# SwiGLU feed-forward on one core: the last store, 128 rows by 128 columns, split by rows over two issuing queues

## The chip, the cores and the metric

The kernel runs on one core of a Trainium2 chip. The metric is device time in microseconds (us) of one execution; the median over several runs is used. A core has engines that run side by side, each with its own queue of instructions: TensorE (PE in the profile) for matrix products, VectorE (DVE), ScalarE (ACT), GpSimd (POOL) and SyncE (SP). SyncE and ScalarE issue the data transfers (DMAs) here; the 16 DMA engines of the core move the data. Engines wait for each other by counting semaphores.

## The reference

```python
B, S, D, F = 1, 2048, 512, 1376        # all bfloat16

def reference(x, w_gate, w_up, w_down):
    g = silu(x @ w_gate)
    u = x @ w_up
    return (g * u) @ w_down            # out: 1 x 2048 x 512
```

## The kernel before

The 2048 tokens are worked on in four chunks of 512, the hidden dimension F in ten blocks of 128 and a rest of 96. Tokens lie along the free dimension of `xT_sb`, so that the first two products come out transposed, hidden units on the 128 partitions. Weights are loaded in slabs by SyncE, the first by ScalarE, in an order written out by hand. At the start SyncE (`loads_on_sync`, L123) and ScalarE (`loads_on_scalar`, L119) issue their first loads at the same time.

For each chunk and block TensorE makes the gate and the up product in two of the eight PSUM banks (L324); ScalarE takes silu of the first (L288), VectorE multiplies by the second into `hT_sb` (L296). The rests of 96 are handled in groups "X" and "Y" of their own (L404).

Then comes the down product. The 16 output tiles of 128 tokens and 512 columns are made in four groups of four (`strips`, L419, matmuls at L442). The last group is finished tile by tile in the loop at L469, matmuls at L481. A tile's bank is copied to one of eight buffers `o_sb`, by VectorE (L300) or ScalarE (L288), in turns, and stored from there to `out_dram` (L257).

The very last tile, `at == NST - 1`, is cut by columns into three groups: 0 to 383 (`LASTA` = 384), 384 to 447 (`LASTB` = 448) and 448 to 511. ScalarE copies the first, VectorE the other two. Two stores carry the tile out: columns 0 to 383 by ScalarE behind its own copy, and columns 384 to 511 by SyncE behind VectorE's last copy. All other output stores are SyncE's.

Planning code makes a list `stores`; each entry has the owner ("S" or "A"), the tile, the columns, the buffer, and the engine and count of the copy to wait for. `store_tiles` (L253) goes through the list for one owner: wait for the copy, issue the DMA, which raises `s_out[ob]` by 16 when it has landed. `n_store[ob]` counts the stores of a buffer, for two uses: a copy into a buffer waits until the buffer's earlier stores have landed, and SyncE ends the program with waits for all of them (L262 and L263). ScalarE's stores come after all its copies (L289), at the end of its queue.

Of the kernel before, what the change touches and what calls it, by code (L numbers as in the profile page):

```python
# [14 lines left out]
def bass_standalone__swiglu_ffn__prompt_kernel(nc, x, w_gate, w_up, w_down, out):  # L15
    _, S, D = x.shape
    F = w_gate.shape[1]
    P = 128
# [7 lines left out]
    NST = S // P  # L26
    LASTA = 384
    LASTB = 448
# [22 lines left out]
    with ExitStack() as es:  # L51
# [15 lines left out]
        o_sb = [sb(f"o_sb{i}", [P, D], BF16) for i in range(NOS)]  # L67
# [13 lines left out]
        s_out = [sem(f"s_out{i}") for i in range(NOS)]  # L81
# [34 lines left out]
        def out_rows(t):  # L116
            return of[t * P:(t + 1) * P, :]
# [35 lines left out]
        def add_group(kind, **what):  # L153
            g = dict(kind=kind, at=len(groups), bank=banks[len(groups) % NB], readers=[], **what)
            groups.append(g)
            return g

        def add_op(eng, g, **what):
            n_read[eng] += 1
            op = dict(g=g, at=n_read[eng], **what)  # L160
            (act_ops if eng == "A" else dve_ops).append(op)
            g["readers"].append((eng, op["at"]))
            return op

        def tview(i, dk):
            return banks[KD * i + dk][:, 0:P // 2].bitcast(BF16)
# [47 lines left out]
        for i in range(NXN):  # L214
            for dk in range(KD):
                eng = "DA"[dk % 2]
                op = add_op(
                    eng, dict(readers=[]), kind="copy", ready=(s_X, KD * i + dk + 1),
                    out=xT_sb[:, dk, i * P:(i + 1) * P], src=tview(i, dk), stored=(None, 0),
                )  # L220
# [8 lines left out]
        NO = len(groups)  # L229
        stores = []  # L230
        n_store = [0] * NOS
        tiles = [c * TPC + q for q in range(TPC) for c in ORDER]
        for at, t in enumerate(tiles):
            ob = at % NOS
            need = 16 * n_store[ob]
            parts = [(0, D)] if at < NST - 1 else [(0, LASTA), (LASTA, LASTB), (LASTB, D)]
            for c0, c1 in parts:
                g = add_group("O", t=t, c0=c0, c1=c1)
                eng = "A" if at % 2 == 1 and c0 == 0 else "D"
                op = add_op(  # L240
                    eng, g, kind="copy", out=o_sb[ob][:, c0:c1], src=g["bank"][:, 0:c1 - c0],
                    stored=(s_out[ob], need),
                )
                if c1 in (LASTA, D):
                    own = "A" if c1 == LASTA else "S"
                    stores.append((own, t, LASTA if c0 == LASTB else c0, c1, ob, eng, op["at"]))
                    n_store[ob] += 1


        def ready(op):  # L250
            return op["ready"] if "ready" in op else (s_P, op["g"]["at"] + 1)

        def store_tiles(eng, own):  # L253
            for o, t, c0, c1, ob, copied, n in stores:
                if o == own:
                    eng.wait_ge(s_A if copied == "A" else s_D, n)
                    eng.dma_start(out_rows(t)[:, c0:c1], o_sb[ob][:, c0:c1]).then_inc(s_out[ob], 16)  # L257

        def on_sync(sp):
            loads_on_sync(sp)  # L260
            store_tiles(sp, "S")
            for i in range(NOS):  # L262
                sp.wait_ge(s_out[i], 16 * n_store[i])  # L263
# [11 lines left out]
        def on_scalar(act):  # L275
            loads_on_scalar(act)
            act.activation(adummy[:, 0:4], zero_c, ACT.Silu)  # L277
            for op in act_ops:
                act.wait_ge(*ready(op))
                if op["kind"] == "silu":  # L280
                    if op["free"]:
                        act.wait_ge(s_D, op["free"])
                    fn = ACT.Silu
                else:
                    if op["stored"][1]:
                        act.wait_ge(*op["stored"])
                    fn = ACT.Copy
                act.activation(op["out"], op["src"], fn).then_inc(s_A, 1)  # L288
            store_tiles(act, "A")  # L289
# [230 lines left out]
```

## Time and profile before

| | us |
|---|---|
| median of 3 runs | 119.98 |
| lowest and highest run | 119.94 and 120.01 |
| the profiled execution, its time | 119.89 |
| its span, first to last instruction | 118.6 |
| TensorE busy | 115.9 (98% of the span) |
| VectorE busy | 38.0 |
| ScalarE busy | 35.1 |

The span is what the profile's rows lie in; the execution's own time is 1.29 us longer than it. The granted clock of TensorE was 1.000 throughout. All rows come from the one profiled execution; times in them count from the start of the span. "SPq" and "ACTq" are the DMA issues of SyncE and ScalarE: the length in such a row is what the issue takes on the issuing engine's queue, not the time until the data has landed.

### The profile page before, as it was taken

The page shows a single profiled execution, that of the slowest core. Times are in us where ns is not written, and L with a number is a line of the kernel's source. Part 1 is how long each engine was busy: PE and PEld are TensorE (multiplying, and loading weights), DVE is VectorE, ACT ScalarE, POOL GpSimd, SP SyncE. Part 2 cuts the span into 40 slices and gives each one's busy share as a digit, 9 for nine tenths or more (in the row PEclk, how much of TensorE's full clock was granted, in tenths as well). Part 3 has the DMA queues.
Part 4 walks back from the last instruction along what each step waited for, and adds up shares of the span by engine and source line. Part 5 has one row for each costly group of instructions (what it writes and reads, how often), then busy time and mean ns, then how long its engine had stood idle before and what let it go on. Part 6 is the DMA issues. An engine that isn't in the chain of part 4 may idle for free.

```text
span 118.6 us, 2344 instructions
## 1 busy us (share of the span) xinstructions
PE 115.9 (98%) x1019; PEld 59.7 (50%) x1019; DVE 38.0 (32%) x60; ACT 35.1 (30%) x62; POOL 1.1 (1%) x7
## 2 busy tenths in 40 slices
PE   7999999999999999999999999999999999999993
PEld 2788444444444444444444444444444445885442
DVE  0206542444433444324444244360000044003321
ACT  3407334353244272343263432330000033003021
POOL 1000000000000000000000000010000000000000
PEclk9999999999999999999999999999999999999999
DMA  3999999991000000000000000000000017200612
GB/s 87 290 186 336 296 161 221 268 357 25 0 6 0 0 0 0 0 3 3 0 0 6 0 0 0 0 0 6 0 6 0 0 57 237 70 0 6 202 64 88
DMA packets 17642, 8.83 MB, mean 74 GB/s; under 512 B 10624, under 2 KB 17632, under 8 KB 17632
## 3 DMA queue, kind: packets, MB, share of 16 engines
q1 hardware_dynamic: 16816, 8.33, 27.3%
q10 hardware_dynamic: 816, 0.36, 1.1%
q8 instruction: 8, 0.13, 0.5%
q14 instruction: 2, 0.02, 0.0%
HBM read 4.75 MB, written 2.10 MB: 58 GB/s over the span
## 4 chain that ended last, share of the span: by engine, by line
PE 98%; DVE 0%; issue 0%
PE bank L324 62%; PE bank L442 25%; PE bank L481 7%; PE bank L356 2%; PE bank L404 2%; PE bank L365 1%; DVE o_sb L300 0%
## 5 line engine op out<-in xcount | busy, mean ns | idle before, releaser
L324 PE MATMUL bank<-xT_sb,w_sb 128*128 128x512 bf16 (+2 forms) x384 | 73.3, 352 | 0.1
L324 PEld LDWEIGHTS bank<-xT_sb,w_sb 128*128 128x128 bf16 x384 | 36.2, 98 | 36.8 <-DMA w_sb<-in_w_gate_dram 0.3
L296 DVE TENSOR_TENSOR hT_sb<-sg_sb,bank 128x512 bf16<-128x512 f32 x40 | 27.5, 688 | 40.2 <-PE bank L324 39.3
L288 ACT ACTIVATE sg_sb<-bank 128x512 f32<-128x512 f32 x40 | 23.9, 597 | 40.6 <-PE bank L324 40.5
L442 PE MATMUL bank<-wd_sb,hT_sb 32*128 32x512 bf16 x496 | 29.0, 374 | 0.0
L442 PEld LDWEIGHTS bank<-wd_sb,hT_sb 32*128 32x128 bf16 x496 | 15.2, 93 | 11.6 <-issue 0.4
L300 DVE CAST o_sb<-bank 128x512 bf16<-128x512 f32 (+1 forms) x10 | 5.7, 595 | 31.1 <-PE bank L442 25.9
L288 ACT ACTIVATE o_sb<-bank 128x512 bf16<-128x512 f32 (+1 forms) x8 | 4.3, 582 | 33.6 <-PE bank L442 27.9
L481 PE MATMUL bank<-wd_sb,hT_sb 128*128 128x512 bf16 (+2 forms) x56 | 8.1, 304 | 0.0
L481 PEld LDWEIGHTS bank<-wd_sb,hT_sb 128*128 128x128 bf16 x56 | 4.2, 98 | 4.2 <-issue 0.4
L442 PE MATMUL bank<-wd_sb,hy_sb 32*128 32x512 bf16 (+1 forms) x32 | 5.0, 371 | 0.0
L296 DVE TENSOR_TENSOR hx_sb<-sgx_sb,bank 32x512 bf16<-32x512 f32 x4 | 2.8, 692 | 3.5 <-ACT sgx_sb L288 3.5
L288 ACT ACTIVATE sgx_sb<-bank 32x512 f32<-32x512 f32 x4 | 2.4, 588 | 4.5 <-PE bank L324 4.5
L356 PE MATMUL bank<-const-bfloat16-1.0 128*128 128x512 bf16 (+1 forms) x9 | 2.8, 463 | 0.8 <-PEq L505 0.8
L442 PE MATMUL bank<-wd_sb,hx_sb 32*128 32x512 bf16 (+1 forms) x16 | 3.0, 371 | 0.0
L288 ACT ACTIVATE sgy_sb<-bank 64x512 f32<-64x512 f32 x4 | 2.4, 590 | 0.1
L356 PEld LDWEIGHTS bank<-const-bfloat16-1.0 128*128 128x128 bf16 x9 | 1.0, 128 | 2.2 <-issue 2.2
L300 DVE COPY xT_sb<-bank 128x128 bf16<-128x128 bf16 x4 | 0.8, 222 | 4.3 <-PE bank L365 4.3
L404 PE MATMUL bank<-xT_sb,w_sb 128*64 128x512 bf16 x16 | 1.9, 382 | 0.0
L442 PEld LDWEIGHTS bank<-wd_sb,hy_sb 32*128 32x128 bf16 x32 | 1.6, 93 | 0.6
L277 ACT ACT_TABLE_LOAD x1 | 1.3, 1283 | 1.9 <-issue 1.9
L404 PEld LDWEIGHTS bank<-xT_sb,w_sb 128*64 128x64 bf16 x16 | 0.8, 109 | 1.0 <-DVE hT_sb L296 0.4
(15 smaller groups left out, 6.6 us busy)
## 6 DMA issues: line engine op xcount, KB each, us to landing
out_dram<-o_sb SPq DMA_DIRECT2D x15, 128.0 KB, 1.8
wd_sb<-in_w_down_dram SPq DMA_DIRECT2D x1, 1280.0 KB, 7.3
w_sb<-in_w_gate_dram SPq DMA_DIRECT2D x1, 480.0 KB, 5.5
w_sb<-in_w_up_dram SPq DMA_DIRECT2D x1, 448.0 KB, 6.2
w_sb<-in_w_gate_dram SPq DMA_DIRECT2D x1, 384.0 KB, 4.3
w_sb<-in_w_up_dram SPq DMA_DIRECT2D x1, 384.0 KB, 4.7
w_sb<-in_w_up_dram SPq DMA_DIRECT2D x2, 128.0 KB, 3.2
w_sb<-in_w_gate_dram SPq DMA_DIRECT2D x1, 256.0 KB, 3.6
```

What stands on the lines that cost most here:

```text
L277: act.activation(adummy[:, 0:4], zero_c, ACT.Silu)
L288: act.activation(op["out"], op["src"], fn).then_inc(s_A, 1)
L296: ins = dve.tensor_tensor(op["out"], op["a"], op["b"], ALU.mult)
L300: ins = dve.tensor_copy(op["out"], op["src"])
L324: return pe.matmul(bank[:, n0:n1], lhsT=w_sb[:, dk, col:col + P], rhs=xT_sb[:, dk, c * SC + n0:c * SC + n1], start=(dk == 0), stop=(dk == ...
L356: pe.matmul(banks[NB - 1][:, 0:width], lhsT=ones_w, rhs=ones_m[:, 0:width], start=True, stop=True)
L365: pe.matmul(tview(i, dk), lhsT=xn_sb[:, i, dk * P:(dk + 1) * P], rhs=ident[:, :], start=True, stop=True, is_transpose=True,).then_inc(s_X, 1)
L404: ins = pe.matmul(g["bank"][y0:y1, :], lhsT=w_sb[:, dk, YC0:YC0 + 64], rhs=xT_sb[:, dk, c * SC:(c + 1) * SC], start=(dk == 0), stop=(dk == ...
L442: ins = pe.matmul(g["bank"][:, 0:c1 - c0], lhsT=h, rhs=wd_sb[r0:r0 + SR, w, c0:c1], start=(start and fk == fks[0]), stop=(stop and fk == f ...
L481: ins = pe.matmul(g["bank"][:, 0:c1 - c0], lhsT=h, rhs=w, start=(last and fk == 0), stop=(fk == (NFF if last else NFF - 1)), skip_group_ch ...
```

## The change

The last tile's store of columns 384 to 511 was one DMA of 128 rows by SyncE. It becomes two: rows 0 to 63 by SyncE, rows 64 to 127 by ScalarE. Both wait for VectorE's last copy. On ScalarE the new store stands behind the store of columns 0 to 383. `n_store` of that buffer grows by one, so that the last wait is for 48 counts in place of 32. Other stores stay as they were: all 128 rows, by the engine that had them. In the new file the store line L257 becomes L264, and the final wait L263 becomes L270.

```diff
+        def halves(at, c0):
+            if at < NST - 1:
+                return [("S", 0, P)]
+            return [("A", 0, P)] if c0 == 0 else [("S", 0, P // 2), ("A", P // 2, P)]
+
         tiles = [c * TPC + q for q in range(TPC) for c in ORDER]
...
                 if c1 in (LASTA, D):
-                    own = "A" if c1 == LASTA else "S"
-                    stores.append((own, t, LASTA if c0 == LASTB else c0, c1, ob, eng, op["at"]))
-                    n_store[ob] += 1
+                    b0 = LASTA if c0 == LASTB else c0
+                    for own, r0, r1 in halves(at, c0):
+                        stores.append((own, t, b0, c1, ob, eng, op["at"], r0, r1))
+                        n_store[ob] += 1
...
         def store_tiles(eng, own):
-            for o, t, c0, c1, ob, copied, n in stores:
+            for o, t, c0, c1, ob, copied, n, r0, r1 in stores:
                 if o == own:
                     eng.wait_ge(s_A if copied == "A" else s_D, n)
-                    eng.dma_start(out_rows(t)[:, c0:c1], o_sb[ob][:, c0:c1]).then_inc(s_out[ob], 16)
+                    eng.dma_start(out_rows(t)[r0:r1, c0:c1], o_sb[ob][r0:r1, c0:c1]).then_inc(s_out[ob], 16)
```

## The prediction

> **What bounds the kernel now.** I read the page first, then the chain of waits over the last microseconds, then the timeline, the SP queue's waits and the DMA packets of the same stretch. Last I looked up the rows elsewhere in the run that resemble the new situation.
>
> The page gives the span and the whole-run chain:
>
> ```profile
> span 118.6 us, 2344 instructions
> ...
> PE 98%; DVE 0%; issue 0%
> ```
>
> TensorE sets 98% of the chain, so nothing but the short tail behind its last matmul can answer to this change. The chain over 116 to 119 us ends so (start, length, what):
>
> ```profile
> 116.83 0.02 issue
> 116.85 0.23 DVE o_sb L300
> ```
>
> The chain of compute ends with VectorE's last copy at 117.08 us. The remaining 1.5 us up to 118.6 is a store. The timeline from 116.6 us shows its order:
>
> ```profile
> 116.20 0.49 ACT L288 ACTIVATE o_sb<-bank 128x384 bf16<-128x384 f32 x1 [2.81 <-PE bank L481]
> ...
> 116.53 0.55 DVE L300 CAST o_sb<-bank 128x64 bf16<-128x64 f32 x2 [1.09 <-PE bank L481]
> ...
> 116.72 0.35 ACTq L257 DMA_DIRECT2D out_dram<-o_sb  x1
> 117.10 0.33 SPq L257 DMA_DIRECT2D out_dram<-o_sb  x1
> ```
>
> ScalarE issues the 384-column store from 116.72 to 117.07. SyncE issues the 128-column store from 117.10, 0.02 us behind the copy. The last wait is SyncE's, for that store, from the waits of the SP queue from 117 us on:
>
> ```profile
> SPq L263 <- DMA out_dram<-o_sb: 0.9, 1, 0.9
> ```
>
> The DMA view says how long each takes to land (page, part 6: KB, us from issue to landing), and, over 117.5 to 118.3 us, what its packets occupy (packets, MB, share of 16 engines):
>
> ```profile
> out_dram<-o_sb ACTq DMA_DIRECT2D x1, 96.0 KB, 1.7
> ...
> out_dram<-o_sb SPq DMA_DIRECT2D x1, 32.0 KB, 1.5
> ```
>
> ```profile
> q10 hardware_dynamic: 144, 0.10, 39.0%
> q1 hardware_dynamic: 144, 0.03, 18.8%
> ```
>
> q10 is ScalarE's queue, q1 SyncE's. Each store is 144 packets: 128 rows, and 16 of 4 bytes that raise the semaphore; nine per DMA engine. One q1 packet takes 0.188 x 16 x 0.8 us / 144 = 16.7 ns. Narrowing the window until no packet is left puts the first q10 packet at 117.57, the first q1 packet at 117.95 and the last one at 118.21.
>
> So the path is: issue 117.10 to 117.43 (0.33), 0.52 to the first packet, 0.26 of packets, 0.37 until the last count has landed (117.10 + 1.48 = 118.58), then the end at 118.6. Of 1.48 us, only 0.26 is moving data.
>
> **What the change does, step by step.** Nothing ahead of 117.08 moves: the matmuls, the three copies and the 384-column store keep their order. SyncE's issue starts as before and is one instruction as before. ScalarE gains one wait, on VectorE's count, and one DMA issue; both are the last things on its queue, so nothing stands behind the wait. The 384-column store is ahead of them and doesn't move. SyncE's last wait asks for 48 counts instead of 32, in the same instruction, priced at nothing. The finish is the later of two halves.
>
> *SyncE's half.* It saves four of its nine packets on each engine: 4 x 16.7 ns = 0.07 us. It would land at 118.51 if its issue stays 0.33. It is not what ends last.
>
> *ScalarE's half, start.* Its queue is free at 117.07, and the copy ends at 117.08, so the issue starts at about 117.10 like SyncE's. The 0.35 us of the earlier issue is hidden by VectorE's copy, with 0.03 us to spare; each 0.1 us more on that issue would cost about 0.07 us here.
>
> *ScalarE's half, issue.* This is the unknown. Two things differ from SyncE's store of before: it follows another issue on its own queue at once, and SyncE issues at the same instant. Rows from the timeline, SP then ACT, for a lone issue, a second one in a row twice, and the two pairs of the start of the run:
>
> ```profile
> 113.42 0.33 SPq L257 DMA_DIRECT2D out_dram<-o_sb  x1
> ...
> 96.83 0.43 SPq L257 DMA_DIRECT2D out_dram<-o_sb  x1
> ...
> 109.85 0.64 SPq L257 DMA_DIRECT2D out_dram<-o_sb  x1
> ...
> 0.81 0.40 SPq L114 DMA_DIRECT2D xn_sb<-in_x_dram  x1
> 1.27 0.42 SPq L99 DMA_DIRECT2D w_sb<-in_w_up_dram  x1
> ```
>
> ```profile
> 0.81 0.47 ACTq L99 DMA_DIRECT2D w_sb<-in_w_gate_dram  x1
> 1.31 0.54 ACTq L114 DMA_DIRECT2D xn_sb<-in_x_dram  x1
> ```
>
> Alone an issue takes 0.33; behind another on its queue 0.43 (once 0.64); beside one of the other queue 0.40 and 0.47. The ScalarE issue at 1.31 has both conditions, and took 0.54. Row count hardly enters: the w_down loads at 23.13 us (32 rows) and 24.51 us (96 rows) both took 0.42. I take 0.54, with bounds 0.33 and 0.76 (SyncE's 0.33 in full, then 0.43).
>
> The Trainium skill, Perfetto Trace Analysis, section DMA Instruction — HWDGE, says that the block that makes descriptors is locked for one issuer at a time and that the profiled duration includes the wait for the lock. Read strictly, that gives the upper bound; the pair at 0.81 lasted 0.40 and 0.47, not 0.33 and 0.68, so this trace agrees at most in part.
>
> *ScalarE's half, the rest.* 0.52 to the first packet, as after the SyncE issue (and 0.50 after ScalarE's own, 117.07 to 117.57). Then 0.26 - 0.07 = 0.19 of packets: the 384-column store's are done by then (last at about 118.03), and SyncE's half, at 117.95 to 118.14, too. If the issue takes no longer than SyncE's, the halves meet on the same 16 engines and the saving shrinks to nothing: ten packets per engine (8 rows, 2 counts) against nine, +0.02. Then 0.37 to landing, as before.
>
> The Trainium skill, DMA: Bandwidth & Descriptors, section Rules for kernel authors, advises against two transfers to disjoint partition halves, since both spread over the same 16 engines. By that rule the 0.07 saving falls away and the sum is +0.21 instead of +0.14. The trace does show q1 and q10 packets mixed on the engines (nine q1 packets before 117.97, while q10 still runs), but in the sum the halves come 0.2 us apart.
>
> **Sum.** Old: 117.10 + 0.33 + 0.52 + 0.26 + 0.37 = 118.58. New: 117.10 + 0.54 + 0.52 + 0.19 + 0.37 = 118.72, or +0.14 us. The profiled execution took 119.89 us, 1.29 outside the span, which I leave alone: 120.03. The median of the runs is 119.98, 0.09 above it, so the median becomes 120.12. With issues of 0.43 and 0.64 the same sum gives +0.03 and +0.24: 120.01 to 120.22. About 0.2% (0.24 us) is what a measurement of this kernel can tell from no change, so this case lies within it.
>
> **The rivals.**
>
> *The issues queue behind each other (slower).* ScalarE's second issue waits until SyncE's is through, 0.33, and then takes 0.35 to 0.43: 0.68 to 0.76. The gain of 0.07 stays. That is +0.28 to +0.36: 120.26 to 120.34, middle 120.32. It decides once the ScalarE issue exceeds 0.33 + 0.07 + 0.24 = 0.64. For it: the ScalarE rows of the start are the longer ones of both pairs, and the first q10 packet there came only at 2.23, the first q1 packet at 1.86, though both were issued at 0.81; a lag of 0.37 in place of my 0.21 gives +0.30. Against: at 2.23 the first engines had just finished SyncE's load (the window to 2.22 holds q1 alone), so that lag can be a queue on the engines, which 64 rows of 16.7 ns don't make. The Trainium skill's lock, above, is this case.
>
> *The halves are free (no change).* The second issue takes 0.33 to 0.35 as at 116.72, beside SyncE's at 117.10. Then -0.07 to +0.02: 119.91 to 120.00, middle 119.97. For it: the late issues, 0.38 us apart on two queues, show no mutual cost (0.35 and 0.33). Against: they don't overlap, and each overlapping or back-to-back row is longer.
>
> *The latency shrinks with the rows (faster).* If half of the 0.52 behind the issue went with the rows, 0.26 + 0.07 = 0.33 us would be saved: 119.65. No row has a lone 64-row transfer, so it can't be excluded; but stores of 1024, 768 and 256 bytes a row all start 0.50 to 0.52 behind their issue, and issue times don't follow the rows.
>
> **How the numbers follow.** Forecast case 0.40, queued issues 0.37, free halves 0.17, shrinking latency 0.06. The forecast is the likeliest case's 120.12. The range 119.91 to 120.37 takes in the first three with their bounds and leaves out the last, and delays beyond the strict queue. Faster by over 0.2%: the last case, 0.06. Slower by over 0.2% (above 120.22): the queue case and the upper edge of the forecast's own range, 0.37 + 0.02 = 0.39. Within: 0.55.
>
> **What would show it.** In the changed profile: an ACTq issue of L264 (the store line there) at about 117.10 with about 0.54, beside an SPq issue of 0.33 to 0.40; 80 packets each for the halves; first q10 packets of the half at about 118.16; SyncE's last wait longer by 0.14. An ACTq issue of 0.68 or more shows the queue case, one of 0.35 the free case. A first packet that comes much under 0.50 behind the issue shows latency that shrinks with rows. The prediction is wrong if the landing, 0.37 behind the last packet, changes, for I left it as it is, or if anything ahead of 117.08 moves.

## The result and the profile after

The changed kernel takes 120.66 us (median of 20 runs, 120.45 to 121.44); the kernel before, run beside it, 120.22 us (median of 20, 119.88 to 120.74). The ratio, that of the means (120.80 and 120.26) and therefore not the quotient of the medians, is 1.0045, with a 95% interval of 1.0028 to 1.0061: slower by 0.34 to 0.73 us. The forecast was +0.14, inside what a measurement can tell from no change. The result lies outside that, on the slow side.

The page and the last lines of the chain from 116 us on:

```profile
span 119.3 us, 2337 instructions
```

```profile
116.94 0.02 issue
116.96 0.22 DVE o_sb L307
```

VectorE's last copy ends at 117.18 instead of 117.08. That 0.11 us is not the change's: in this execution the chain at the start of the run ran through the load of the second block of `xn_sb`, which landed later (its last count at 4.66 us, 4.37 before), and in the profiles below the end of this copy lies anywhere from 117.10 to 118.01. So I count the tail from the end of this copy. The timeline of the issues behind it:

```profile
116.83 0.36 ACTq L264 DMA_DIRECT2D out_dram<-o_sb  x1
117.21 0.53 SPq L264 DMA_DIRECT2D out_dram<-o_sb  x1
117.24 0.55 ACTq L264 DMA_DIRECT2D out_dram<-o_sb  x1
```

and SyncE's last wait, and the DMA view over 117.5 to 119.3 us (busy tenths in 40 slices of 0.045 us; KB and us to landing):

```profile
SPq L270 <- DMA out_dram<-o_sb: 1.3, 1, 1.3
```

```profile
DMA  0000368998963000000135520136420000000000
...
out_dram<-o_sb SPq DMA_DIRECT2D x1, 16.0 KB, 1.8
out_dram<-o_sb ACTq DMA_DIRECT2D x1, 16.0 KB, 2.0
```

The half-size stores take longer to land (1.8 and 2.0 us) than the whole one did (1.5). Both issues are long, SyncE's too, though its queue was idle. The slices show three separate bursts: the 384-column store, then SyncE's half, then ScalarE's. Between the first two the DMA engines do nothing for about 0.25 us. They are not the bottleneck; the halves come to them late. Of ScalarE's half nothing moves before 118.65, though its issue ended at 117.79: up to there the DMA view has packets of SyncE's queue alone, from there on those of ScalarE's (windows 118.2 to 118.65 and 118.65 to 119.3).

```profile
q1 hardware_dynamic: 80, 0.02, 19.4%
```

```profile
q10 hardware_dynamic: 80, 0.02, 12.9%
```

With the packet and landing records of the trace, the path of the store that lands last, term by term:

| term, us | before | after | difference | forecast |
|---|---|---|---|---|
| last copy to issue | 0.03 | 0.05 | +0.03 | 0 |
| issue | 0.332 | 0.551 | +0.22 | +0.21 |
| end of issue to first packet | 0.515 | 0.872 | +0.36 | 0 |
| first packet to end of last | 0.265 | 0.228 | -0.04 | -0.07 |
| end of last packet to last count | 0.366 | 0.353 | -0.01 | 0 |
| last copy to last count | 1.505 | 2.057 | +0.55 | +0.14 |

The +0.55 us agrees with the ratio (0.0045 x 120.2 = 0.54). SyncE's half took 0.525 to issue and 0.654 from there to its first packet.

### The profile page after: what moved, and what is told of

It is laid out like the page before. It is cut to its first block, busy times and chain, and to the rows that moved or that the text cites. A ratio compares the mean times of both kernels' runs of the same rounds, so it can differ in the third digit from the quotient of the medians.

```text
span 119.3 us, 2337 instructions
## 1 busy us (share of the span) xinstructions
PE 115.4 (97%) x1011; PEld 59.9 (50%) x1019; DVE 38.0 (32%) x60; ACT 35.1 (29%) x62; POOL 1.1 (1%) x7
## 4 chain that ended last, share of the span: by engine, by line
PE 94%; DMA 3%; issue 1%; ACTq 0%; DVE 0%
PE bank L331 60%; PE bank L449 25%; PE bank L488 7%; DMA xn_sb<-in_x_dram 3%; PE bank L411 2%; ACTq L99 0%; PE bank L372 0%; DVE o_sb L307 0%
## 5 line engine op out<-in xcount | busy, mean ns | idle before, releaser
L449 PEld LDWEIGHTS bank<-wd_sb,hT_sb 32*128 32x128 bf16 x496 | 15.3, 93 | 11.5 <-issue 0.4
```

Source lines behind the costliest of these rows:

```text
L449: ins = pe.matmul(g["bank"][:, 0:c1 - c0], lhsT=h, rhs=wd_sb[r0:r0 + SR, w, c0:c1], start=(start and fk == fks[0]), stop=(stop and fk == f ...
```

## The experiments

"Tail" is the time from the end of VectorE's last copy to the last landed count: 1.505 us before, 2.057 after. The first four runs set three explanations against each other: overlap of issues on two queues, the 64-row shape, and a second issue on ScalarE's own queue.

**Whole stores that meet.** In the kernel before:

```diff
                     eng.wait_ge(s_A if copied == "A" else s_D, n)
+                    if o == "A":
+                        eng.wait_ge(s_D, n_read["D"])
```

> The kernel before, unsplit, but ScalarE's 384-column store also waits for VectorE's last copy, so that its issue and SyncE's start together, 128 rows each. Theory 'overlap' (two issues that overlap on the two queues slow each other, whatever their rows): SyncE's issue 0.50 to 0.55 us instead of 0.33, its first packet 0.65 behind the end of the issue instead of 0.52; ScalarE's issue 0.47 to 0.55 and its first packet 0.87 behind it; last landing 2.0 to 2.2 us behind VectorE's last copy (1.50 before). Rival 'shape' (a store of 64 rows is the dear thing) and rival 'own queue' (a second issue right behind another on ScalarE's queue is): 0.33 and 0.35, 0.52 and 0.50 behind, last landing about 1.6 us behind the copy, only some packets in the way.

The timeline:

```profile
117.96 0.33 SPq L259 DMA_DIRECT2D out_dram<-o_sb  x1
118.02 0.35 ACTq L259 DMA_DIRECT2D out_dram<-o_sb  x1
```

The issues overlap and neither grows; first packets came 0.50 and 0.53 behind them. Overlap of two whole stores costs 0.03 at most. The tail is 1.79, since the 96 KB of ScalarE's store now come last, and the ratio 1.0042 (1.0020 to 1.0064).

**The halves without the 384-column store.**

```diff
-            return [("A", 0, P)] if c0 == 0 else [("S", 0, P // 2), ("A", P // 2, P)]
+            return [] if c0 == 0 else [("S", 0, P // 2), ("A", P // 2, P)]
```

> The changed kernel without ScalarE's store of columns 0 to 383 of the last 128 rows; that part of the output is not written. The two halves still meet, but no issue stands ahead of them on ScalarE's queue. 'Overlap': as in the changed kernel, issues of 0.47 to 0.55 us, first packets 0.65 and 0.87 us behind them, last landing 1.95 to 2.05 us behind the last copy. 'Own queue': ScalarE's half falls to 0.35 and 0.52, last landing about 1.45. 'Shape': both halves stay as slow as in the changed kernel, as for 'overlap', since both have 64 rows.

Issues of 0.52 and 0.56, first packets 0.65 and 0.88 behind, tail 2.06, ratio 1.0054 (1.0033 to 1.0076): as in the changed kernel, so the issue ahead on ScalarE's queue is not the cause. The explanation by ScalarE's own queue falls.

**Both halves by SyncE.** `("A", P // 2, P)` becomes `("S", P // 2, P)`.

> Both halves by SyncE, one behind the other, so that no two queues issue at once. 'Overlap': the first half is as cheap as a lone issue (0.33 us, first packet 0.52 behind), the second like a second one on a queue (0.43, then 0.52); last landing 0.03+0.33+0.04+0.43+0.52+0.2+0.36 = 1.9 us behind the last copy. 'Shape': the first half already takes 0.53 and 0.65, the second lands at 2.2 us or later. 'Own queue': as 'overlap' here.

The rows of SyncE's stores in the last 2 us (duration min/median/max):

```profile
L264 SPq DMA_DIRECT2D out_dram<-o_sb x2: 524/560/596, 118.0 to 118.6; - x2
```

With nothing else issuing, the first half already takes 0.524 and its first packet comes 0.66 behind. The tail is 2.43, +0.93; the ratio 1.0106 (1.0086 to 1.0126) is a little more than that, 1.03 us or above, and the rest is not explained. The shape is dear by itself.

**The halves apart.**

```diff
+                    if o == "A" and r0 > 0:
+                        for i in range(2):
+                            eng.activation(adummy[:, 4 * i:4 * i + 4], zero_c, ACT.Copy).then_inc(s_A, 1)
+                            eng.wait_ge(s_A, n_read["A"] + i + 1)
```

> The changed kernel, but ScalarE does two small activations (4 columns of a spare tile, about 0.2 us each with a wait for each) between VectorE's last copy and the issue of its half, so that the issue starts 0.45 to 0.6 us behind SyncE's. 'Overlap': SyncE's half returns to 0.33 and 0.52, ScalarE's issue to 0.35 and 0.52, and although it starts 0.5 us later the last landing comes no later than in the changed kernel: 0.55+0.35+0.52+0.2+0.36 = 2.0 us behind the last copy, against 2.06. 'Shape' and 'own queue': ScalarE's half stays at 0.55 and 0.87 and the whole delay is added, 2.5 us.

```profile
117.24 0.52 SPq L268 DMA_DIRECT2D out_dram<-o_sb  x1
...
117.74 0.54 ACTq L268 DMA_DIRECT2D out_dram<-o_sb  x1
```

SyncE's half doesn't get cheaper (0.52, 0.66 behind), against "overlap". ScalarE's issue stays at 0.54, but its first packet comes 0.65 behind instead of 0.87. The tail is 2.30, between the two forecasts: of the 0.48 us of delay, 0.24 came back. So there are two effects: a 64-row store costs 0.19 more in the issue and 0.14 more behind it, and of two that meet, the second costs a further 0.22. The ratio is 1.0071 (1.0048 to 1.0094).

The next four ask what about the half is dear: being a part, having 64 rows, or having few bytes.

**96 and 32 rows, 112 and 16 rows, apart.** The kernel above with other row bounds, `("S", 0, 96), ("A", 96, P)` and `("S", 0, 112), ("A", 112, P)`.

> The run with the halves apart (two small activations ahead of ScalarE's part), but SyncE stores rows 0 to 95 and ScalarE rows 96 to 127. Theory 'part' (any store of fewer than all 128 rows is dear): both issues 0.50 to 0.55 us, first packets 0.65 behind, last landing 2.25 us behind VectorE's last copy. Rival '64' (only the 64-row form is; the loads of 32 and 96 rows at 23 to 25 us took 0.42 behind one another, those of 64 rows 0.68 to 0.99): both issues 0.33 to 0.36, first packets 0.50 to 0.52 behind, last landing 1.95 us behind. Rival 'bytes' (a small transfer is dear): the 8 KB part of ScalarE dear, 0.53 or more, the 24 KB part in between.

> The same with rows 0 to 111 by SyncE and 112 to 127 by ScalarE. 'Part': both 0.50 to 0.55 and 0.65 behind, last landing 2.2 us behind the last copy. '64': 0.33 to 0.36 and 0.52, last landing 1.9. 'Bytes': ScalarE's 4 KB the dearest of all, SyncE's 28 KB close to 0.33.

The timeline of the first:

```profile
117.32 0.33 SPq L268 DMA_DIRECT2D out_dram<-o_sb  x1
...
117.82 0.35 ACTq L268 DMA_DIRECT2D out_dram<-o_sb  x1
```

and the same 0.33 and 0.35 in the second; all four first packets came 0.50 to 0.51 behind. The tails are 1.92 and 1.90, as "64" had it, in spite of the 0.5 us of delay; the ratios 1.0035 (1.0012 to 1.0058) and 1.0037 (1.0015 to 1.0058). Rows of 96, 112, 32 and 16 cost what 128 cost.

**By columns.** SyncE columns 448 to 511, ScalarE 384 to 447, all 128 rows:

```diff
...
+                        for own, x0, x1 in (("S", LASTB, D), ("A", LASTA, LASTB)):
+                            stores.append((own, t, x0, x1, ob, eng, op["at"], 0, P))
+                            n_store[ob] += 1
```

> The last 128 columns split by columns instead of rows, to the same two engines behind the same copy: SyncE columns 448 to 511, ScalarE 384 to 447, all 128 rows each, 16 KB each as in the changed kernel. 'Part' and '64': SyncE's issue 0.33, ScalarE's 0.35 to 0.45, first packets about 0.52 behind, last landing 1.5 to 1.65 us behind the last copy, time within 0.2% of before. 'Bytes': as slow as the changed kernel, 0.52 and 0.55, 2.0 us or more. If issues that meet cost something with 128 rows too, ScalarE's first packet comes 0.7 us or more behind its issue.

Issues of 0.33 and 0.44 for 16 KB each: few bytes are not dear. The first packets came 0.52 and 0.50 behind. But the tail was 1.70, not 1.5 to 1.65, and the ratio 1.0026 (1.0007 to 1.0046). The last packet had ended at 1.23, earlier than its landing would suggest. That is a new cost; see below.

**The tile ahead in two halves of 64 rows by 512 columns, the last store whole.** `halves` returns `[("S", 0, P // 2), ("S", P // 2, P)]` for tile `NST - 2`.

> The last tile as before (one 128-row store of 128 columns by SyncE), but the tile ahead of it stored as two halves of 64 rows by 512 columns, both by SyncE, at about 115.5 us, off the critical path. 'Part' and '64': their issues take 0.52 and about 0.6 us, first packet of the first 0.65 behind it, although each moves 64 KB. 'Bytes': 0.33 and 0.43, and 0.50. The time within 0.2% of before in any case, since SyncE is free again at about 116.7, before it is needed at 117.1.

```profile
115.88 0.52 SPq L266 DMA_DIRECT2D out_dram<-o_sb  x1
...
116.44 0.60 SPq L266 DMA_DIRECT2D out_dram<-o_sb  x1
```

First packets 0.66 and 0.65 behind: the same price with 64 KB each. Off the path it costs nothing (tail 1.53, ratio 0.9994, 0.9971 to 1.0016).

Then the change itself without the 64-row form, no delay:

**96 and 32 rows, 80 and 48 rows, meeting.** `("S", 0, 96), ("A", 96, P)` and `("S", 0, 80), ("A", 80, P)` in the changed kernel.

> The change itself with other row counts, and no delay: SyncE rows 0 to 95, ScalarE rows 96 to 127, both right behind VectorE's last copy. Theory '64' (only the 64-row form is dear, and only issues of that form slow each other): SyncE's issue 0.33, ScalarE's, second on its queue, 0.44, first packets 0.51 behind each, last landing 0.03+0.44+0.51+0.18+0.36 = 1.52 us behind the last copy, the time within 0.2% of before. Rival 'meeting' (any two issues at once slow each other, so that 0.2 of the 0.55 would stay): ScalarE's first packet 0.7 or more behind its issue, last landing 1.75.

> The same with rows 0 to 79 and 80 to 127 (5 and 3 rows for each of 16 DMA engines). '64': as in the run with 96 and 32 rows, 0.33 and 0.44 for the issues, last landing 1.52 to 1.55 us behind the last copy, the time within 0.2% of before. If more row counts than 64 are dear, these two, not tried so far, may show 0.52 and 0.65 again; 'meeting': 1.75.

The timeline of the first:

```profile
117.14 0.33 SPq L264 DMA_DIRECT2D out_dram<-o_sb  x1
117.16 0.44 ACTq L264 DMA_DIRECT2D out_dram<-o_sb  x1
```

0.33 and 0.44 in the second too. ScalarE's first packets came 0.52 and 0.50 behind the issue. The 64-row cost is gone: of the 0.55, 0.36 went. Yet both tails are 1.70 instead of the 1.52 expected, although the last packets had ended at 1.17 and 1.19. The ratios are 1.0005 (0.9988 to 1.0021) and 1.0015 (0.9998 to 1.0033): the 0.19 that is left cannot be told from nothing in one comparison.

**64 rows meet 32.** `[("S", 0, 64), ("A", 64, 96), ("S", 96, P)]`.

> SyncE stores rows 0 to 63 and behind them rows 96 to 127, ScalarE rows 64 to 95; a 64-row issue meets a 32-row one. SyncE's first issue 0.52, first packet 0.65 behind, in either case. If the dear form holds up the other queue too, ScalarE's issue is longer than 0.44, or its first packet later than 0.52 behind it, by about 0.2 in all; if only two dear forms slow each other, 0.44 and 0.51. SyncE's second part is issued at about +0.57 us and lands last, about 2.0 us behind the copy.

```profile
117.45 0.52 SPq L264 DMA_DIRECT2D out_dram<-o_sb  x1
117.46 0.44 ACTq L264 DMA_DIRECT2D out_dram<-o_sb  x1
```

ScalarE's first packet came 0.50 behind. Its 32-row store feels nothing of the 64-row one beside it; of the pairs tried, only two 64-row stores slow each other. The kernel ran once, so only its trace counts. The tail is 2.21, not about 2.0: SyncE's second part took 0.58 to issue although it has 32 rows. A store behind a 64-row one is dear too, as the first load of 32 rows behind those of 64 is in the kernel before.

The last runs ask where the 0.19 us of the other splits comes from. In all three (columns, 96 and 32, 80 and 48), counts land without a gap from 1.11 to 1.70, 48 in 0.59 us, one per 12 ns; before, 32 in 0.39.

**A semaphore of its own for the third store**, number 121:

```diff
-                    eng.dma_start(out_rows(t)[r0:r1, c0:c1], o_sb[ob][r0:r1, c0:c1]).then_inc(s_out[ob], 16)
+                    eng.dma_start(out_rows(t)[r0:r1, c0:c1], o_sb[ob][r0:r1, c0:c1]).then_inc(
+                        s_out[ob] if r0 == 0 else s_last, 16)
...
+            sp.wait_ge(s_last, 16)
```

> The 96 and 32 row split again, but ScalarE's 32-row store raises a semaphore of its own (number 121; the other two stores of the tile stay on 113). Theory 'counting' (counts of one semaphore arrive one after another, about 12 ns each, so that 48 take 0.59 us from the first, at 1.11 us behind the last copy): the last landing comes at 1.50 to 1.54 us behind the copy instead of 1.70, 0.35 to 0.37 behind the last packet. Rival 'receipt' (writes from both queues mixed on the DMA engines simply take 0.53 to be confirmed): 1.70 again.

Tail 1.71, ratio 1.0006 (0.9986 to 1.0025). My "counting" theory, a queue on one semaphore, fell. The rival "receipt" had the 1.70. But if mixed writes as such took longer to be confirmed, both parts would land late alike; in the trace the 32 counts on 113 ended at 1.54, and the 16 on 121 ran from 1.51 to 1.71, one set behind the other.

**Another semaphore number for all three, and for both of the whole version.** In both, `.then_inc(s_out[ob] if t != tiles[-1] else s_last, 16)` with number 119 for `s_last`.

> The 96 and 32 row split, all three stores of the last tile on one semaphore, but number 119 instead of 113. In the traces the steps between counts were 11.7 ns on 113, 13.3 on 112, 10 on 106, 5 on 109 and 2.5 on 119. If the step goes with the number, 48 counts at 2.5 ns hold nothing up and the last landing comes at 1.50 to 1.54 us; if every semaphore counts alike once 48 arrive, 1.70 as before. 'Receipt': 1.70.

> The kernel before, whole 128-row last store, with both stores of the last tile on semaphore 119. 'Counting': 32 counts of 12.3 ns from 1.11 us end at 1.505 us behind the copy, which is what was seen; freed of it, the last landing comes 0.34 to 0.37 behind the last packet's start at 1.13, that is 1.47 to 1.50: a gain of 0.00 to 0.035 us, seen in the trace only. 'Receipt': 1.50.

The tails are 1.65 (against 1.70; one count per 11.6 ns, not 2.5) and 1.49 (against 1.505). The number matters little: the short steps on 119 belonged to a load, and the 10 and 5 ns on 106 and 109 the commonest of uneven steps. On average the counts of every whole store of the kernel before, on all eight numbers, landed 11.5 to 13.9 ns apart, but for one at 18.4. Ratios 1.0011 (0.9989 to 1.0033) and 0.9996 (0.9975 to 1.0017).

**No 96 KB store ahead, and eight rows instead of 32.** `return [] if c0 == 0 else [("S", 0, 96), ("A", 96, P)]`, and `("S", 0, 112), ("A", 112, 120)`.

> The 96 and 32 row split without ScalarE's store of columns 0 to 383 of the last 128 rows (that part of the output is not written), so that the DMA engines carry nothing else. Theory 'pace' (completion counts of stores pass one behind the other, about 12 ns each, whatever their semaphore): SyncE's first counts land at about 1.30 us behind the last copy, and 32 of them take 0.37 to 0.39, so 1.67 to 1.69 us, although the last packet leaves at about 1.1. If the delay of the other splits came from the data of the 96 KB store ahead: last landing 0.37 behind the last packet, 1.45 us.

> SyncE stores rows 0 to 111, ScalarE rows 112 to 119; rows 120 to 127 of the last 128 columns are not written. Eight rows go over eight DMA engines, one row each, so that eight counts come from packets instead of 16. 'Pace': 40 counts of 12.2 ns from 1.11 us, so 1.60 us behind the last copy. If each further store costs 0.19 whatever its counts: 1.70; if only the last packet matters: 1.50.

```profile
117.42 0.33 SPq L264 DMA_DIRECT2D out_dram<-o_sb  x1
117.42 0.38 ACTq L264 DMA_DIRECT2D out_dram<-o_sb  x1
```

```profile
117.12 0.33 SPq L264 DMA_DIRECT2D out_dram<-o_sb  x1
117.14 0.59 ACTq L264 DMA_DIRECT2D out_dram<-o_sb  x1
```

Each ran once, so only the traces count. Without the large store the tail is 1.66 (forecast 1.67 to 1.69), its 32 counts landing from 1.29 on, although the last packet ended at 1.17. With 40 counts it is 1.64, between the 1.60 of "pace" and the 1.70 of a fixed price, although the last packets ended at 1.12. Both go better by the number of counts than by the last packet or the data ahead. So, as far as these traces show, completions of these stores pass one at a time, about 12 ns each, whichever semaphore they raise. Whether it is the count or the confirmation of the write before it that takes the 12 ns is open; the 16 counts of two loads of the kernel before landed 4.7 and 4.1 ns apart, so a count alone can pass faster. That the pace shows in the times, and not only in the traces, rests on the four splits with three whole sets of counts and no 64 rows (columns, 96/32, 80/48, own semaphore): their ratios average 1.0013, or 0.16 us, near the 0.19, though the intervals of three of the four take in no change.

No version lands usefully before the kernel before: the best is 0.016 us ahead in the trace, on another semaphore number, and cannot be told from it in time.

## Why the prediction was wrong

**Right:** nothing ahead of the last copy moved by the change; ScalarE's half ended last; the DMA engines and the landing (0.353 against 0.366) were as priced; and no gain came from latency that shrinks with rows. The path of issue, first packet, packets and landing was the right one to add up. Of the 0.54 us by which the measured 120.66 exceeds the forecast 120.12, 0.24 is not the change's: the kernel before, run beside it, took 120.22, and I had started from 119.98.

**The step that failed** is "0.52 to the first packet, as after the SyncE issue": it was 0.87. Of the 0.36 missing, 0.14 is the price of a 64-row store by itself, and 0.22 that two of them met. This one term is 0.36 of the 0.41 us by which the path fell short.

**Right by accident** is the issue. I took 0.54, from a row where an issue follows another and meets a third; it took 0.55. The runs show that those two conditions give 0.44, as with 96 and 32 rows, and that 64 rows alone give 0.52 to 0.54. The number came out by luck.

The root is one sentence: "Row count hardly enters", with the loads of 32 and 96 rows as witnesses. A little ahead of them, in the same block of loads, the kernel before has the very row count that the change introduces. Its timeline:

```profile
20.86 0.68 SPq L142 DMA_DIRECT2D wd_sb<-in_w_down_dram  x1
```

```profile
21.59 0.87 SPq L142 DMA_DIRECT2D wd_sb<-in_w_down_dram  x1
22.50 0.58 SPq L144 DMA_DIRECT2D wd_sb<-in_w_down_dram  x1
```

against 0.42 for the next ones of 32 rows. The two loads of L142 have 64 rows; the one at 22.50 has 32, right behind them. I had seen these rows and left them out. Read by shape, they would have set another price: 0.26 to 0.45 more in the issue than 0.42, less 0.07 of packets, +0.19 to +0.38 even without the part behind the issue.

**The rivals.** "The issues queue behind each other" had the sign right and the mechanism wrong: whole stores that meet take 0.33 and 0.35, and a 32-row issue beside a 64-row one 0.44. Of the pairs tried, only two 64-row stores hold each other up, and mostly behind the issue (+0.22), not in it (0.55 against 0.54). The lag of the first q10 packet at the start of the run, which I set aside, is no proof of a queue of issues either, since whole stores that meet show no such lag. The Trainium skill, Perfetto Trace Analysis, section DMA Instruction — HWDGE, counts a wait for a lock into the profiled duration; these rows show none of it, whole stores least of all. "The halves are free" holds for no split: without the 64 rows the issue side is nearly free, but a further set of counts that lands together with another costs 0.19, which I had "priced at nothing". In the changed kernel itself this cost does not show, since the halves land one after the other (landing 0.353). "Latency shrinks with the rows" fell: 0.50 to 0.51 for 16 to 112 rows. With eight rows the first packet came 0.33 behind the issue, but that issue was longer, and from its start it took 0.91, against 0.94 and 0.96 for 48 and 32 rows. Two middles in the prediction are off by 0.01 or 0.02 (120.26 to 120.34 has 120.30, 119.91 to 120.00 has 119.96); nothing hangs on them.

The Trainium skill, DMA: Bandwidth & Descriptors, section Rules for kernel authors, advises one whole transfer instead of two halves. The runs agree in the outcome: every split of the last store landed later than the whole one (1.64 to 2.43 against 1.505). Its reason, shared DMA engines, is not what cost here: with 96 and 32 rows the packets of both ended 1.17 us behind the copy against 1.14.

## What to carry to other kernels

Price a new transfer from the row that has its exact shape, and take a row that doesn't fit the rule for a finding before taking it for a disturbance. A last store of 32 KB is nearly all fixed latency (0.27 of 1.51 us was moving data), so splitting it can save little and buys a second issue and a further set of completions. If a store must be split by rows, compare other row counts: here 96 and 32 rows landed 0.36 us earlier in the trace than 64 and 64.

## What was not expected of the hardware

- A store of 64 rows, with no other issue at the same time or right ahead: issue 0.52 to 0.54 us, first packet 0.65 to 0.66 behind; of 16, 32, 96, 112 and 128 rows 0.33 to 0.36 and 0.50 to 0.52. It did not matter whether a row had 256 or 1024 bytes, nor which queue issued it. Why 64 is special stays open.
- Two such stores issued together: the second one's first packet 0.87 to 0.88 behind its issue.
- Where the completion counts of the last stores landed without a gap, they came 11.6 to 13.2 ns apart on average, on one semaphore or two: 32 in 0.37 to 0.41 us, 40 in 0.52, 48 in 0.55 to 0.59.
- An issue of eight rows took 0.59 us, against 0.44 for 32 or 48 rows in the same place; its first packet came no later for it.
